# Softmax sums: the reciprocal is taken before the turn, the turn stands between the two ranges of value products, and the scaling is ordered two row minima later

## The chip, the cores and the metric

The kernel runs on one core of one Trainium2 chip. The metric is the device time of one execution in microseconds (us). The engines: TensorE (PE; PEld is its weight load), VectorE (DVE), ScalarE (ACT), GpSimd (POOL), and SyncE (SP), whose queue issues all DMA transfers of this kernel. Each engine works its own instructions in the order in which they stand; an instruction that waits holds up what stands behind it on the same engine. [...]

## The reference

Attention for 4 batches, 8 heads, 576 positions and head size 64, with a decay bias made from running sums of `s`; then a gated feed-forward block with a spatial mixing matrix (moe1); then a channel-mix block (moe2). Cut to what matters here:

```python
scores = scale * q @ k.T                       # per batch and head: 576 x 576
cum = cumsum(maximum(s, 0))
scores = where(causal, -1e9, scores + minimum(-(cum[:, None] - cum[None, :]), 0))
scores = scores - scores.max(-1)
attn = exp(scores)
attn = attn / (attn.sum(-1) + 1e-9)            # the division that the change touches
x = attn @ v                                   # heads side by side: 512 columns
# moe1, per batch
h = gelu(x @ w_in); u, v = halves of h
v = layernorm(v) * g_ln
x = x + (u * (w_sg @ v + b_sg)) @ w_out
# moe2, over all tokens
k = relu(mix(x, mu_k) @ w_k); r = sigmoid(mix(x, mu_r) @ w_r)
out = r * ((k * k) @ w_v)
```

The kernel keeps x transposed (features on the partitions), so the row sums of the softmax divide along the free axis, and each needs to be spread over 64 partitions.

## The kernel before, in words

**Attention.** Heads are worked in 16 pairs; pair `pr` holds heads 2hp and 2hp+1 of batch b. The generator `attn_pair` loads q and k of each head (`kq`), splits them into a rounded part and a rest (so that a product takes two matmuls, L252 and L253), and then goes through nine score steps `(hh, i)`: (0,0) to (0,3) are the four 128-row blocks of the first head, (2,4) the last 64 rows of both heads together, (1,0) to (1,3) the second head. In a step PE writes the scores into a PSUM tile `sc` (two buffers), DVE adds the mask and takes the row minimum `mx` in one instruction (L277; its small second row reads the accumulator), ACT takes the exponential and writes the row's sum into a column of `sums` (L285), PE turns the block by matmuls with the identity into a PSUM tile `tp` (three buffers), and ACT or DVE copies it to `pt1` or `pt2` (L305 to L314). Since there are two `sc` buffers, the scores of step n+2 wait for the row minimum of step n.

**The division.** After the nine steps PE turns `sums` (128 rows, 9 columns) into `rt` (9 rows, 128 columns, L317), DVE adds 1e-9 (L319) and takes the reciprocal (L320), SP stores it to DRAM (`rdram`, L321) and loads it three times, broadcast over 64 partitions, into `rb` (128 x 576, L324 to L326). PE meanwhile computes the two ranges of value products `pv` (L338): range 0 is queries 0 to 255, range 1 queries 256 to 575; ACT copies each to `xT` (L340). DVE's multiplication of `xT` by `rb` (L352) is put off: `scale_pending` issues it during the next pair, after the row minimum of step `LATE`, here (0, 3), or at the start of a batch's moe1 for the pair that is its last.

**moe1 and moe2.** moe1 of batch b reads the four scaled `xT` of its batch (L386 to L389) and runs groups of matmuls (L368), named v, u, sg and o after what they compute; `wc`, `wcs`, `wy` are tiles of its weights and of their splitting on DVE and ACT. Its yields are interleaved with the attention of the batches ahead, so that from 60 to about 380 us most of PE's attention steps stand among moe1's matmuls. After it, moe2 (k, r, and products psa to psc) needs no attention.

**What sets the order.** The program's text gives one order; the framework's scheduler then reorders the instructions of each engine by its own estimates, with priorities, buffers and dependences as constraints. A change at one place can so move instructions of many others.

Of the kernel before, what the change touches and what calls it, by code (L numbers as in the profile page):

```python
# [8 lines left out]
F32 = mybir.dt.float32  # L9
# [5 lines left out]
B, H, S, D = 4, 8, 576, 64  # L15
DM, DFF = 512, 1024
FH = DFF // 2
P = 128
# [10 lines left out]
SUM_EPS = 1e-9  # L29
# [8 lines left out]
def fused_kernel(ctx, tc, kqT, vL, s, w_in, g_ln, w_sgT, b_sg, w_out, mu_k, mu_r, w_k, w_v, w_r, out):  # L38
    nc = tc.nc
# [10 lines left out]
    rdram = dram.tile([B * H // 2, 9, P], F32, tag="rdram", name="rdram")  # L50
    ident = const.tile([P, P], F32, tag="ident", name="ident")
# [43 lines left out]
    psum1 = banks1.enter_context(tc.tile_pool(name="psum1", bufs=3, space=bass.MemoryType.PSUM))  # L95
# [3 lines left out]
    at = ap_stack.enter_context(tc.tile_pool(name="at", bufs=2, side="right"))  # L99
# [16 lines left out]
    with tc.high_priority():  # L116
# [20 lines left out]
        out=mask[:, 512:], in_=mask[:, 512:], pattern=[[-1, P]], compare_op=ALU.is_ge,  # L137
# [70 lines left out]
    def attn_pair(b, hp):  # L208
        pr = b * (H // 2) + hp
        first = b == 0  # L210
        ops = []
        for hh in range(2):
# [5 lines left out]
            i = hd % (NSET + 1) if first else hd % NSET  # L218
# [25 lines left out]
        sm = sums[pr % 2]  # L244
# [12 lines left out]
        for hh, i in steps:  # L257
# [8 lines left out]
            for ci, (c0, c1) in enumerate(chunks):  # L266
# [5 lines left out]
                else:  # L272
# [5 lines left out]
                    out=st[:, c0:c1], in0=sc[:, :n], in1=mk, op0=ALU.add, op1=ALU.min,  # L278
# [10 lines left out]
            exps.append(e)  # L289
            if (hh, i) == LATE:  # L290
                scale_pending(mi)
# [5 lines left out]
            tag = "acc" if first and i > 2 else "tp"  # L297
            tp = psum1.tile([P, 512], F32, tag=tag, name=f"tp{pr}_{hh}_{i}", bufs=3)
# [14 lines left out]
                    nc.scalar.copy(pt2[:, a, :4, q0 - QS:], tp.rearrange("p (j a m) -> p a j m", j=4, a=2)[:, a])  # L313
                nc.vector.tensor_copy(pt2[:, :, 3, 0:64], tp4[:, :P].rearrange("p (a m) -> p a m", a=2))  # L314
            yield (i + 1) * 200
        rt = psum1.tile([P, 512], F32, tag="tp", name=f"rt{pr}", bufs=3)
        nc.tensor.transpose(rt[:9, :P], sm, ident)  # L317
        rc = at.tile([9, P], F32, tag="rc", name=f"rc{pr}")
        nc.vector.tensor_scalar_add(rc, rt[:9, :P], SUM_EPS)  # L319
        nc.vector.reciprocal(rc, rc)  # L320
        nc.sync.dma_start(out=rdram[pr], in_=rc)  # L321
        rbs = at.tile([P, S], F32, tag="rb", name=f"rb{pr}", bufs=2)
        rq = rdram[pr].rearrange("i q -> (i q)")
        nc.sync.dma_start(out=rbs[:64], in_=rq[:S].partition_broadcast(64))  # L324
        nc.sync.dma_start(out=rbs[64:, :512], in_=rq[S + 64:].partition_broadcast(64))
        nc.sync.dma_start(out=rbs[64:, 512:], in_=rq[S:S + 64].partition_broadcast(64))  # L326
        for r in range(2):
            q0, n = ((0, QS), (QS, S - QS))[r]
            acc = psum1.tile([P, 512], F32, tag="acc", name=f"pv{pr}_{r}", bufs=3)
            nk = 2 if r == 0 else NT  # L330
            for kk in range(nk):
                o = max(0, kk * P - q0)
                for a in range(2):
                    if r == 0:
                        pt = pt1[:, a, :QS] if kk == 0 else pt1[:, a, QS:]
                    else:
                        pt = pt2[:, a, kk, o:] if kk < 4 else pt2[:, a, 3, 0:64]
                    nc.tensor.matmul(acc[64 * a:64 * a + 64, o:n], vf[:, a, kk], pt, start=(kk == 0), stop=(kk == nk - 1))  # L338

            nc.scalar.copy(x_t[:, q0:q0 + n], acc[:, :n])  # L340
            yield 4000
# [6 lines left out]
    def scale_pending(early):  # L348

        while pending:  # L350
            x_t, rbs = pending.pop()
            i = nc.vector.tensor_tensor(out=x_t, in0=x_t, in1=rbs, op=ALU.mult)  # L352
            if early is not None:
                after(i, early)
# [156 lines left out]


    pairs = [attn_pair(b, h) for b in range(B) for h in range(H // 2)]

    def a_stream():
# [4 lines left out]
                yield total  # L520
            yield 2 * n + 2.0

    LATE = (0, 3)
    A_COST = 2 * 3136 + 6600 + 8000 + 128
    E_COST = V_W * 56 * 512 + U_W * 8 * 12 * 288 + O_W * 8 * 12 * 288 + S_W * 8 * 14 * 288
    LEAD = 1
# [334 lines left out]
```

## Time and profile before

| | |
|---|---|
| median of 3 runs | 683.07 us (681.43 to 684.61) |
| the profiled execution | 684.48 us, span 682.7 us, mean granted clock 0.988 |
| PE busy | 645.9 us (95%), 3912 matmuls |
| DVE busy | 478.4 us (70%), 995 instructions |
| ACT busy | 415.9 us (61%), 940 instructions |
| POOL busy | 220.1 us (32%), 233 instructions |

Shares are of the span. The span leaves out 1.8 us around the first and the last instruction of the profiled execution. The chain that ended last is 77% PE and 8% DVE. The kernel has three stretches with a different limit: attention alone up to about 60 us, attention among moe1's matmuls up to about 380 us, and matmuls without attention after it.

### The profile page before, as it was taken

Reading aid. Unit: us, or ns where it says so; the run is one execution under the profiler, and the core shown is the slowest. Engines: PE = TensorE matmul, PEld = TensorE weight load, DVE = VectorE, ACT = ScalarE, POOL = GpSimd, SP = SyncE. Lnnn points to the kernel's source line nnn. Section 1 sums busy time; section 2 is a strip of 40 time slices with the busy share of each in tenths; the row PEclk is TensorE's granted clock in tenths of the full one; section 3 lists DMA queues with packets and bytes.
Section 4 is the critical chain, followed back from the end, with each engine's and each line's share of the span. In section 5 each row is a group of like instructions: output and inputs, shape, how many; then the busy total and the mean of one; then the engine's idle time right before and its main releaser. Section 6 shows DMA issues by size and latency. Waiting matters only on the chain.

```text
span 682.7 us, 11530 instructions
## 1 busy us (share of the span) xinstructions
PE 645.9 (95%) x3912; PEld 554.7 (81%) x3912; DVE 478.4 (70%) x995; ACT 415.9 (61%) x940; POOL 220.1 (32%) x233
## 2 busy tenths in 40 slices
PE   2879999899999999999999998999999999999997
PEld 1557676779978988877988898988888988999997
DVE  6876679986568645479543488777865969677773
ACT  4978777785458656268633374577754778543430
POOL 8556646368437468247462030000000000000000
PEclk9979999999999999999999999999999999999999
DMA  7764662454553532833511764566745594455643
GB/s 218 216 207 144 180 169 76 142 162 149 161 185 90 163 93 55 263 91 103 152 33 49 254 229 142 170 212 224 249 143 184 169 359 152 160 187 179 238 139 116
DMA packets 56459, 112.74 MB, mean 165 GB/s; under 512 B 7680, under 2 KB 20624, under 8 KB 56400
## 3 DMA queue, kind: packets, MB, share of 16 engines
q1 hardware_dynamic: 56400, 112.01, 52.0%
q8 instruction: 31, 0.51, 0.3%
q14 instruction: 28, 0.23, 0.1%
HBM read 74.46 MB, written 28.02 MB: 150 GB/s over the span
## 4 chain that ended last, share of the span: by engine, by line
PE 77%; DVE 8%; DMA 7%; ACT 2%; issue 2%; SPq 2%; POOL 1%; DVEq 0%; ACTq 0%; POOLq 0%
PE k L368 15%; PE sg L368 9%; PE r L368 7%; PE pv L338 7%; PE psa L770 7%; PE o L368 5%; PE tp L303 5%; PE u L368 4%; PE sc L252 4%; PE v L368 4%; PE psb L770 4%; PE sc L253 3%; DMA lraw<-in_w_k_dram 2%; PE psc L770 2%; DMA kq<-in_kqT_dram 2%
## 5 line engine op out<-in xcount | busy, mean ns | idle before, releaser
L368 PE MATMUL k<-x,wk 128*128 128x512 f32 (+1 forms) x480 | 101.4, 372 | 0.0
L368 PEld LDWEIGHTS k<-x,wk 128*128 128x128 f32 x480 | 83.6, 188 | 17.4
L252 PE MATMUL sc<-ka,qa 128*128 128x512 f32 (+3 forms) x180 | 63.6, 363 | 23.2 <-DMA ka<-ka 12.4
L285 ACT ACTIVATE st<-st,mx 128x128 f32<-128x128 f32 (+4 forms) x124 | 72.0, 582 | 19.8 <-DVE mx L277 19.2
L277 DVE CUSTOM_DVE_ANT_0 st<-sc,mask 128x512 f32<-128x512 f32 (+3 forms) x124 | 61.0, 502 | 27.8 <-PE sc L253 24.6
L368 PE MATMUL sg<-wsg,vn 128*128 128x288 f32 x448 | 67.0, 303 | 3.5 <-DVE vn L69 2.6
L368 PEld LDWEIGHTS sg<-wsg,vn 128*128 128x128 f32 x448 | 62.3, 192 | 4.3 <-DVE vn L69 2.9
L338 PE MATMUL pv<-pt,vf 128*64 128x320 f32 (+4 forms) x448 | 64.7, 366 | 0.2 <-ACT pt L305 0.2
L252 PEld LDWEIGHTS sc<-ka,qa 128*128 128x128 f32 x180 | 33.9, 189 | 33.2 <-DVE mx L277 14.4
L253 PE MATMUL sc<-KB,QB 128*128 128x512 f32 (+3 forms) x180 | 57.1, 333 | 0.9 <-DMA KB<-crt 0.9
L338 PEld LDWEIGHTS pv<-pt,vf 128*64 128x64 f32 x448 | 35.4, 136 | 23.5 <-issue 5.2
L303 PE MATMUL tp<-ident,st 128*128 128x128 f32 x300 | 49.5, 282 | 1.6 <-ACT st L285 1.5
L368 PE MATMUL r<-x,wr 128*128 128x512 f32 (+1 forms) x240 | 50.6, 372 | 0.0
L368 PEld LDWEIGHTS r<-x,wr 128*128 128x128 f32 x240 | 41.7, 188 | 8.8
L368 PE MATMUL v<-wv,xs 128*128 128x512 f32 x192 | 48.4, 397 | 0.0
L69 POOL TENSOR_TENSOR qa<-kq,QB 64x576 fp32r<-64x576 f32 x29 | 45.1, 1555 | 4.5 <-ACT QB L229 2.3
L229 POOL CAST QB<-kq 64x576 fp32r<-64x576 f32 x28 | 21.2, 761 | 74.1 <-PE sc L253 44.8
L303 PEld LDWEIGHTS tp<-ident,st 128*128 128x128 f32 x300 | 35.6, 142 | 11.0 <-ACT st L285 5.1
L69 POOL TENSOR_TENSOR KB<-kq,ka 64x576 fp32r<-64x576 f32 x29 | 42.7, 1474 | 3.4 <-ACT ka L230 1.4
L368 PE MATMUL o<-gh,wc 128*128 128x288 f32 x192 | 40.8, 298 | 0.7 <-DMA wc<-wscr 0.7
L368 PEld LDWEIGHTS v<-wv,xs 128*128 128x128 f32 x192 | 35.1, 188 | 7.5 <-POOL QB L229 0.5
L368 PE MATMUL u<-xs,wc 128*128 128x288 f32 x288 | 40.8, 297 | 0.0
(188 smaller groups left out, 1451.3 us busy)
## 6 DMA issues: line engine op xcount, KB each, us to landing
wc<-wscr SPq DMA_DIRECT2D x24, 512.0 KB
kq<-in_kqT_dram SPq DMA_DIRECT2D x32, 288.0 KB
kr<-kdram SPq DMA_DIRECT2D x12, 768.0 KB
kdram<-k SPq DMA_DIRECT2D x16, 512.0 KB
yt<-ydram SPq DMA_DIRECT2D x24, 257.0 KB
vf<-in_vL_dram SPq DMA_DIRECT2D x16, 320.0 KB
ydram<-y SPq DMA_DIRECT2D x16, 288.5 KB
gt<-gdram SPq DMA_DIRECT2D x12, 384.0 KB
```

What stands on the lines that cost most here:

```text
L69: eng.tensor_tensor(out=lo, in0=x, in1=f32(hi), op=ALU.subtract)
L229: (nc.scalar.copy if hd < 2 else nc.gpsimd.tensor_copy)(qb[64:128], kq[64:128])
L252: nc.tensor.matmul(sc[:m, :c1 - c0], qa[:, q], ka[:, c0:c1], start=True, stop=False)
L253: nc.tensor.matmul(sc[:m, :c1 - c0], qb[:, q], kb[:, c0:c1], start=False, stop=True)
L277: mi = nc.vector.tensor_tensor_reduce(out=st[:, c0:c1], in0=sc[:, :n], in1=mk, op0=ALU.add, op1=ALU.min, scale=-SCALE, scalar=mx[:, 0:1] i ...
L285: e = nc.scalar.activation(st[:, :w], st[:, :w], AF.Exp, bias=mx[:, last:last + 1], scale=-1.0, accum_out=sm[:, i + 5 * (hh == 1):i + 5 * ...
L303: nc.tensor.transpose(tp[:, c:c + P], st[:, j * P:(j + 1) * P], ident)
L338: nc.tensor.matmul(acc[64 * a:64 * a + 64, o:n], vf[:, a, kk], pt, start=(kk == 0), stop=(kk == nk - 1))
L368: nc.tensor.matmul(acc, a, w_, start=(i == 0), stop=(i == n - 1))
L770: nc.tensor.matmul(ps[:, c, :HW], l, r, start=(start and i == 0), stop=(i == len(mms) - 1), skip_group_check=True)
```

## The change

Epsilon and reciprocal are now applied to `sums` as it stands, 128 rows by 9 columns (`rs`, new L317 and L318). The new `spread()` has PE turn `rs` (L323), ACT copy the turned tile from PSUM to `rc` (L325, sixteen new ACT instructions in all), and SP store and load as before (L326 to L330). It is called between the two ranges of value products. `LATE` becomes (1, 0): the scaling follows the row minimum of the next pair's step (1, 0), two steps behind (0, 3). Below the change, lines have numbers seven higher (L338 is L345, L352 is L359, L368 is L375, L389 is L396).

```diff
--- before.py
+++ after.py
@@ -313,18 +313,25 @@
                     nc.scalar.copy(pt2[:, a, :4, q0 - QS:], tp.rearrange("p (j a m) -> p a j m", j=4, a=2)[:, a])
                 nc.vector.tensor_copy(pt2[:, :, 3, 0:64], tp4[:, :P].rearrange("p (a m) -> p a m", a=2))
             yield (i + 1) * 200
-        rt = psum1.tile([P, 512], F32, tag="tp", name=f"rt{pr}", bufs=3)
-        nc.tensor.transpose(rt[:9, :P], sm, ident)
-        rc = at.tile([9, P], F32, tag="rc", name=f"rc{pr}")
-        nc.vector.tensor_scalar_add(rc, rt[:9, :P], SUM_EPS)
-        nc.vector.reciprocal(rc, rc)
-        nc.sync.dma_start(out=rdram[pr], in_=rc)
+        rs = at.tile([P, 9], F32, tag="rs", name=f"rs{pr}")
+        nc.vector.tensor_scalar_add(rs, sm, SUM_EPS)
+        nc.vector.reciprocal(rs, rs)
         rbs = at.tile([P, S], F32, tag="rb", name=f"rb{pr}", bufs=2)
-        rq = rdram[pr].rearrange("i q -> (i q)")
-        nc.sync.dma_start(out=rbs[:64], in_=rq[:S].partition_broadcast(64))
-        nc.sync.dma_start(out=rbs[64:, :512], in_=rq[S + 64:].partition_broadcast(64))
-        nc.sync.dma_start(out=rbs[64:, 512:], in_=rq[S:S + 64].partition_broadcast(64))
+
+        def spread():
+            rt = psum1.tile([P, 512], F32, tag="tp", name=f"rt{pr}", bufs=3)
+            nc.tensor.transpose(rt[:9, :P], rs, ident)
+            rc = at.tile([9, P], F32, tag="rc", name=f"rc{pr}")
+            nc.scalar.copy(rc, rt[:9, :P])
+            nc.sync.dma_start(out=rdram[pr], in_=rc)
+            rq = rdram[pr].rearrange("i q -> (i q)")
+            nc.sync.dma_start(out=rbs[:64], in_=rq[:S].partition_broadcast(64))
+            nc.sync.dma_start(out=rbs[64:, :512], in_=rq[S + 64:].partition_broadcast(64))
+            nc.sync.dma_start(out=rbs[64:, 512:], in_=rq[S:S + 64].partition_broadcast(64))
+
         for r in range(2):
+            if r:
+                spread()
             q0, n = ((0, QS), (QS, S - QS))[r]
             acc = psum1.tile([P, 512], F32, tag="acc", name=f"pv{pr}_{r}", bufs=3)
             nk = 2 if r == 0 else NT
@@ -520,7 +527,7 @@
                 yield total
             yield 2 * n + 2.0
 
-    LATE = (0, 3)
+    LATE = (1, 0)
     A_COST = 2 * 3136 + 6600 + 8000 + 128
     E_COST = V_W * 56 * 512 + U_W * 8 * 12 * 288 + O_W * 8 * 12 * 288 + S_W * 8 * 14 * 288
     LEAD = 1
```

The scheduler's orders differ in many places. Three of them follow, and a fourth in words.

On SP, at the end of pair 0: `kq5` is the q and k of head 5, `rdram` the store of the reciprocals of pair 0, `rb0` their three loads, `vf2` the values of pair 2. Before:

```order
L231 DMA qa4_532<-QB1_85 64x576
L321 DMA rdram_65<-rc0_298 9x128
L217 DMA kq5_543<-in_kqT_dram 128x576
L324 DMA rb0_302<-rdram_65 64x576
L325 DMA rb0_302<-rdram_65 64x512
L326 DMA rb0_302<-rdram_65 64x64
```

After:

```order
L231 DMA qa4_536<-QB1_85 64x576
L217 DMA kq5_547<-in_kqT_dram 128x576
L326 DMA rdram_65<-rc0_308 9x128
L239 DMA vf2_544<-in_vL_dram 128x640
L328 DMA rb0_299<-rdram_65 64x576
L329 DMA rb0_299<-rdram_65 64x512
L330 DMA rb0_299<-rdram_65 64x64
```

The load of `kq5` has moved ahead of the store of the reciprocals, and `vf2` between the store and the loads.

On DVE, in pair 4, where pair 3 is scaled (`xT3` by `rb3`; `mx4_2_4` and `mx4_1_0` are row minima of pair 4, `pt2_4` a copy of a turned block). Before:

```order
L277 ISA st4_2_4_948,mx4_2_4_949<-sc4_2_4_1_956,mask2_123,mx4_2_4_949 128x64
L277 ISA mx4_2_4_949 128x1
L307 COPY pt2_4_903<-tp4_0_3_942 128x4x128
L352 TENSOR_TENSOR xT3_708<-xT3_708,rb3_840 128x576
L277 ISA st4_1_0_974,mx4_1_0_975<-sc4_1_0_0_976,mask_83 128x128
L277 ISA mx4_1_0_975 128x1
```

After:

```order
L277 ISA st4_2_4_956,mx4_2_4_957<-sc4_2_4_1_964,mask2_123,mx4_2_4_957 128x64
L277 ISA mx4_2_4_957 128x1
L359 TENSOR_TENSOR xT3_714<-xT3_714,rb3_843 128x576
L307 COPY pt2_4_911<-tp4_0_3_950 128x4x128
L277 ISA st4_1_0_982,mx4_1_0_983<-sc4_1_0_0_984,mask_83 128x128
L277 ISA mx4_1_0_983 128x1
```

The scaling now stands ahead of the copy to `pt2_4`; both still stand ahead of the minimum of step (1, 0), whose row comes after.

On DVE, in pair 6, where pair 5 is scaled (`u0`, `v0`, `vn0` are gates of moe1 of batch 0; `wcs3`, `wcs4`, `wy4_0` weights being split). Before:

```order
L419 TENSOR_SCALAR v0_1022<-v0_1022,mv0_1024,rstd0_1025 64x512
L352 TENSOR_TENSOR xT5_1150<-xT5_1150,rb5_1360 128x576
L82 SCALAR_TENSOR_TENSOR wy4_0_1456<-wr4_0_1455,wy4_0_1456 128x256
L499 SCALAR_TENSOR_TENSOR u0_1_1419<-u0_1_1419,u0_1_1_1437 128x288
L69 TENSOR_TENSOR wcs3_1399<-wy3_1_1410,wcs3_1399 128x256
L84 SCALAR_TENSOR_TENSOR wy4_0_1456<-wy4_0_1456 128x256
L307 COPY pt2_6_1520<-tp6_0_3_1577 128x4x128
L277 ISA st6_2_4_1621,mx6_2_4_1622<-sc6_2_4_1_1629,mask2_123,mx6_2_4_1622 128x64
L277 ISA mx6_2_4_1622 128x1
L277 ISA st6_1_0_1647,mx6_1_0_1648<-sc6_1_0_0_1649,mask_83 128x128
L277 ISA mx6_1_0_1648 128x1
```

After:

```order
L277 ISA mx6_2_4_1633 128x1
L69 TENSOR_TENSOR wcs3_1411<-wy3_1_1422,wcs3_1411 128x256
L84 SCALAR_TENSOR_TENSOR wy4_0_1468<-wy4_0_1468 128x256
L506 SCALAR_TENSOR_TENSOR u0_1_1431<-u0_1_1431,u0_1_0_1432 128x288
L69 TENSOR_TENSOR vn0_0_1034<-v0_1030,vn0_0_1034 64x512
L506 SCALAR_TENSOR_TENSOR u0_1_1431<-u0_1_1431,u0_1_1_1449 128x288
L508 SCALAR_TENSOR_TENSOR u0_1_1431<-u0_1_1431,u0_1_0_1432 128x288
L307 COPY pt2_6_1532<-tp6_0_3_1588 128x4x128
L69 TENSOR_TENSOR wcs4_1466<-wy4_0_1468,wcs4_1466 128x256
L277 ISA st6_1_0_1658,mx6_1_0_1659<-sc6_1_0_0_1660,mask_83 128x128
L277 ISA mx6_1_0_1659 128x1
L359 TENSOR_TENSOR xT5_1160<-xT5_1160,rb5_1367 128x576
```

The second minimum of step (2, 4) (its accumulator read is the first row) has moved ahead of the two weight operations `wcs3` and `wy4_0`; the minimum of step (1, 0) stays behind them and more; the scaling has moved behind that minimum.

On PE, in pair 8, the score steps of the second head stood apart among moe1's o groups of batch 0: `sc8_1_1` and `sc8_1_2` between o0_2_0 and o0_2_1, `sc8_1_3` ahead of v1_0. Now `sc8_1_1` stands in the last o group, `sc8_1_2` and `sc8_1_3` inside v1_0, and the first four score steps of pair 9 follow directly.

## Rows read from the trace of the kernel before

**Rows 1.** Windows: stretch, length, busy us (instructions) per engine; PEclk is the granted clock

```profile
38.00:48.20 10.20, 7.77 (x28) 6.02 (x28) 8.56 (x25) 7.00 (x20) 4.61 (x5) 0.50 0.67 208
...
60.00:96.00 36.00, 35.17 (x228) 24.93 (x226) 24.04 (x68) 28.85 (x82) 18.24 (x17) 1.00 0.55 154
...
96.00:133.50 37.50, 32.72 (x203) 25.72 (x201) 33.59 (x73) 26.61 (x69) 21.24 (x24) 1.00 0.39 114
...
133.50:137.00 3.50, 3.50 (x16) 3.42 (x15) 2.97 (x11) 3.06 (x11) 0.00 (x0) 0.51 0.47 158
...
160.00:380.00 220.00, 219.15 (x1496) 187.32 (x1495) 131.12 (x345) 120.73 (x309) 116.46 (x123) 1.00 0.40 118
```

**Rows 2.** Waits of PE, 20 to 160 us: total us, times, longest

```profile
PE sc L252 <- DVE mx L277: 11.2, 10, 3.3
```

**Rows 3.** Waits of PE, 160 to 680 us

```profile
PE sg L368 <- DVE vn L69: 2.6, 1, 2.6
```

**Rows 4.** Waits of DVE, 20 to 160 us

```profile
DVE xT L352 <- DMA rb<-rdram: 5.1, 5, 2.1
```

**Rows 5.** Groups of DVE by form: busy us, mean ns of one, idle before

```profile
L320 DVE RECIPROCAL rc<-rc 9x128 f32<-9x128 f32 x16 | 15.0, 937 | 0.3
...
L319 DVE TENSOR_SCALAR rc<-rt 9x128 f32<-9x128 f32 x16 | 4.3, 271 | 0.7 <-PE rt L317 0.7
...
L416 DVE BATCH_NORM_AGGREGATE mv<-st 128x2 f32<-128x6 f32 x16 | 2.7, 170 | 0.2
...
L62 DVE TENSOR_SCALAR mu<-mu 128x8 f32<-128x8 f32 x1 | 1.1, 1108 | 1.7 <-DMA mu<-in_mu_r_dram 1.7
```

**Rows 6.** Timeline of SP, pair 0: start us, duration us, line, operation

```profile
31.59 0.31 SPq L321 DMA_DIRECT2D rdram<-rc  x1
...
32.00 0.35 SPq L217 DMA_DIRECT2D kq<-in_kqT_dram  x1
```

**Rows 7.** Timeline of DVE, pairs 0 and 1: start, duration, idle before

```profile
30.62 0.94 DVE L320 RECIPROCAL rc<-rc 9x128 f32<-9x128 f32 x1
...
36.62 0.96 DVE L230 CAST ka_f<-kq 64x576 fp32r<-64x576 f32 x1 [1.21 <-DMA kq<-in_kqT_dram]
...
39.71 1.83 DVE L352 TENSOR_TENSOR xT<-xT,rb 128x576 f32<-128x576 f32 x1 [1.11 <-DMA rb<-rdram]
```

**Rows 8.** Timeline of PE after that

```profile
38.44 0.58 PE L252 MATMUL sc<-ka,qa 128*128 128x256 f32 x1 [2.54 <-DVE mx L277]
...
43.14 0.80 PE L252 MATMUL sc<-ka,qa 128*128 128x512 f32 x1 [1.99 <-DVE mx L277]
```

**Rows 9.** Timeline of ACT, pair 0, the first product copied from PSUM

```profile
31.97 0.38 ACT L340 COPY xT<-pv 128x256 f32<-128x256 f32 x1
```

**Rows 10.** Timeline of DVE, pairs 3 and 4

```profile
79.56 0.69 DVE L307 COPY pt<-tp 128x512 f32<-128x512 f32 x1 [1.56 <-PE tp L303]
...
81.37 0.76 DVE L352 TENSOR_TENSOR xT<-xT,rb 128x576 f32<-128x576 f32 x1 [1.12 <-DMA rb<-rdram]
```

**Rows 11.** Timeline of DVE, pairs 5 and 6

```profile
126.47 0.76 DVE L352 TENSOR_TENSOR xT<-xT,rb 128x576 f32<-128x576 f32 x1 [0.51 <-DMA rb<-rdram]
...
128.33 1.27 DVE L69 TENSOR_TENSOR wcs<-wy,wcs 128x256 fp32r<-128x256 f32 x1
...
129.52 1.61 DVE L84 SCALAR_TENSOR_TENSOR wy<-wy 128x256 uint32<-128x256 uint32 x1
...
131.66 0.27 DVE L277 CUSTOM_DVE_ANT_0 st<-sc,mask,mx 128x64 f32<-128x64 f32 x1
...
133.63 0.42 DVE L69 TENSOR_TENSOR wcs<-wy,wcs 128x256 fp32r<-128x256 f32 x1
```

**Rows 12.** Timeline of POOL beside it

```profile
127.84 1.48 POOL L69 TENSOR_TENSOR KB<-kq,ka 64x576 fp32r<-64x576 f32 x1
...
129.39 1.46 POOL L69 TENSOR_TENSOR qa<-kq,QB 64x576 fp32r<-64x576 f32 x1
```

**Rows 13.** Timeline of PE beside it

```profile
131.99 0.38 PE L252 MATMUL sc<-ka,qa 128*128 128x256 f32 x1 [3.32 <-DVE mx L277]
```

## Prediction

> **What bounds the kernel now.** I read the page's busy shares first, then windows cut where the granted clock or the mix of work changes, then PE's waits, and then timelines around the longest of them. PE is busy for 95% of the span, so a part of VectorE's work can pay only where PE waits for VectorE. The windows show where that is. From 160 to 380 us, where pairs 8 to 15 are worked among moe1's matmuls, PE is busy for 219.15 of 220 us [rows 1]; behind 160 us its longest entry in the waits is 2.6 us, for a tile of moe1 [rows 3]. There even a free division would give at most 0.85 us. From 20 to 160 us PE waits 11.2 us, in ten waits, for the row minimum `mx` [rows 2], and VectorE is busy for 33.59 of 37.5 us between 96 and 133.5 us [rows 1]. Three of the ten make up 2.54 + 1.99 + 3.32 = 7.85 us [rows 8, 13]. Behind two long pauses stand the stretches at half clock, 38 to 48.2 us (granted 0.50) and 133.5 to 137 us (0.51) [rows 1]: PE's pause came first, then the lower level. In 20 to 160 us VectorE also waits 5.1 us, in five waits, for the loads of `rb` [rows 4].
>
> **The change, part by part.** All durations are from the profiled execution, 684.48 us (span 682.7 and 1.8 around it). It is 1.4 us above the median of 683.07; sums are made against 684.48, and 1.4 is taken off at the end.
>
> *The smaller reciprocal.* Each pair loses an addition of 271 ns and a reciprocal of 937 ns on 9 x 128 [rows 5], 1.21 us of VectorE, and gains two operations on 128 x 9. The trace has no such operation. The nearest are 128 x 2 from 128 x 6 at 170 ns, and a single 128 x 8 at 1,108 ns [rows 5]. I take 170 ns, since that is a mean over 16 and the other ran once. The relief is 1.21 - 0.34 = 0.87 us a pair; between the ends it is +0.87 to -1.0 us. Sixteen pairs make 13.9 us of VectorE, but only the seven pairs worked before 160 us (0 to 6) can hand any to PE, 6.1 us at most, and each only if nothing else is late at its next wait.
>
> *The turn between the ranges.* PE's turn now needs `rs`, so it can wait for VectorE; where it stands behind the first range, matmuls already issued cover it. The sixteen copies on ScalarE are new. The first product copied from PSUM, 128 x 256, took 0.38 us [rows 9]; a copy of 9 x 128 lies between nothing and that, I take 0.3 us, 4.8 us in all. ScalarE is busy for 120.73 of 220 us behind 160 us [rows 1], which hides it there. In the early pairs it is also a delay: in pair 0 the new copy stands behind the copy that starts at 31.97 and lasts 0.38 [rows 9], so `rc` is ready at about 32.65 instead of 30.62 + 0.94 = 31.56 [rows 7]. That is 1.1 us later, although VectorE's part is finished sooner. No term for PE follows yet; it returns with the scaling.
>
> *SP at the end of pair 0.* The store of `rc` was issued at 31.59, and the load of `kq5` stood behind it at 32.00 [rows 6]. VectorE then waited 1.21 us for that load, until 36.62 [rows 7], and PE waited 2.54 us for the minimum behind it [rows 8]. The load now stands ahead of the store, so its issue no longer waits for the reciprocals. VectorE's 1.21 us go, and what is late next is VectorE's own queue: -1.2 us on PE's path, bounds 0 and -2.54. The store waits behind one more issue and `vf2` stands before the loads of `rb0`, which adds 0.3 to 0.6 us to them by the issue times [rows 6].
>
> *The scaling of pair 0.* It waited 1.11 us for `rb` and took 1.83 us from 39.71 [rows 7]; then the minimum for which PE waited 1.99 us came [rows 8]. With `rc` 1.1 us later and the scaling one minimum and two weight operations later, `rb` and the scaling are again due together, at about 40.7. I take 0, bounds -1.99 and +1.1.
>
> *The scaling of pair 3.* In the new order it stands ahead of the copy to `pt2_4`, not behind it. VectorE was free at 79.56 - 1.56 = 78.0; the copy ran at 79.56 while the loads travelled, and the scaling ran at 81.37 [rows 10]. Now VectorE waits from 78.0 to about 81.4 for `rb`, then scales, then copies (0.69 us), and the minimum of step (1, 0) comes 0.69 us later, the copy itself 2.6 us. PE has moe1's matmuls there (35.17 of 36 busy [rows 1]) but its order is fixed too: +0.7 us, bounds 0 and +2.6.
>
> *The scaling of pair 5.* It started at 126.47 after a wait of 0.51 us; with other work behind it the second minimum of step (2, 4) came at 131.66, and PE stood for 3.32 us until 131.99 [rows 11, 13]. That minimum now comes before `wcs3` and `wy4_0`, which took 1.27 and 1.61 us [rows 11], so this wait should go. What is late next is the minimum of step (1, 0), for which the scores two steps on wait. The scaling (0.76 + 0.51) has left its path and the relief of pair 5 (0.87) helps, 2.1 us together; but four instructions that ran behind it, from about 132.2 to 133.63 + 0.42 [rows 11], now run ahead of it, 1.9 us. It comes about when it came; PE has done two short steps more by then, but the step after waits for the scaling and one more minimum. I take -0.5 us, bounds -3.32 and +1.5.
>
> *The rest.* The other seven of the ten waits sum to 11.2 - 7.85 = 3.35 us [rows 2], in pieces that mostly end with a row minimum not far behind a division; I take -0.3 us, bounds 0 and -1.7. The closer bunch of score steps in pair 8 takes away some of the matmuls that stood between; PE idles 0.85 us in the whole stretch today [rows 1], so it can only lose: +0.3 us, bounds 0 and +4, the upper end if the two steps moved into v1_0 each wait for a whole exponential chain of about 2 us (scores, minimum and exponential, an estimate).
>
> Sum: -1.2 + 0 + 0 + 0.7 - 0.5 - 0.3 + 0.3 = -1.0. That gives 683.5 against 684.48, and about 682.0 beside the median.
>
> [...] VectorE's `wcs3` took 1.27 us at 128.33 while GpSimd ran tensor operations from 127.84 and 129.39 [rows 11, 12]; the same shape took 0.42 us at 133.63 [rows 11], in a window in which GpSimd did nothing [rows 1]. [...]
>
> **The rivals.**
>
> *The waits fall in a row, 675.* If VectorE's relief adds up over pairs, half of the 11.2 us goes (-5.6). Where a pause shortens, the clock may stay up: at full clock 38 to 48.2 us would take half of PE's 7.77 busy us (3.9) less, and 133.5 to 137 half of 3.5 (1.75) [rows 1]; one of the two, on average 2.8. 684.48 - 8.4 - 1.4 = 674.7. For it: PE's longest pauses end with VectorE. Against: the minimum for step (1, 0) of pair 6 keeps its place in time, and pair 0's scaling too.
>
> *The scaling takes over as the wait, 688.* VectorE works in order, so a scaling whose `rb` is not there holds up the row minima behind it. Its place moved by two minima, but `rc` now comes by way of PE and ScalarE, 1.1 us later in pair 0. Today VectorE waits 5.1 us for `rb` in seven pairs [rows 4]. If each `rb` comes 1.1 us later against its scaling, 7.7 us more are waited; with the 3.4 us of pair 3 and half of it passed on to PE, 5 us, and no relief left: 684.48 + 5 - 1.4 = 688. It decides from the point where waits for `rb` before 160 us exceed about 9 us. For it: rows 10. Against: two minima and their gaps are mostly longer than 1.1 us.
>
> *The change does nothing to PE, 683.* Each pause ends on another VectorE instruction at the same time. The fixed order of moe1's weight work speaks for it, the moved load of `kq5` against it.
>
> *The small operations are stretched by GpSimd, 683.5.* By the overlap seen at 128.33, a VectorE operation that meets GpSimd's lasts 1.27 - 0.42 = 0.85 us more. GpSimd works about half of 20 to 160 us; fourteen small operations, seven of them met, cost 6 us, which eats the 6.1 us of relief, and the later `rc` costs some tenths. For it: `wcs3`. Against: the old reciprocal's mean.
>
> **How the numbers follow.** Forecast 0.40 (its own range 679 to 686), waits falling 0.23, scaling as the wait 0.21, nothing 0.09, stretched 0.07. A change under 0.5%, 3.4 us here, can't be told from none. Faster than 679.7: the second case, and a quarter of the first, 0.33. Slower than 686.5: nearly all of the third and a little of the first, 0.22. Within: 0.45. The range runs from 674.5 to 688, which leaves out half of the two outer cases, about 0.2.
>
> **What would show it.** The row minima's share of PE's waits before 160 us should fall from 11.2 to about 9 us, with the 3.32 us of pair 6 moved on to the next steps. VectorE's busy time should fall by about 14 us, ScalarE's rise by about 5. The pause of 2.54 us should be near 1.3. Waits for `rb` should stand near 8 us before 160 us. The small operations should take 0.17 us each. PE's idle time from 160 to 380 us should stay under 2 us. I am wrong if both stretches at half clock are gone (then it is faster), if PE's idle time grows in pair 3 or 8 by more than 2 us, or if the small operations take near 1 us.

## The result, and the profile after

The changed kernel takes 688.17 us (median of 16 runs, 686.37 to 691.59). The kernel before, run as often beside it, takes 686.51 us (679.59 to 689.79; its first three runs, known ahead of the prediction, had 683.07). The ratio is 1.0054, 95% interval 1.0035 to 1.0073; it is not the quotient of the two medians, which is 1.0024 (that of the means is 1.0044). So the change makes the kernel slower, by 1.7 us between the medians and by 3.7 us by the ratio, where a gain of 1.0 us, to 682.0, was forecast. Of the 6.2 us between 682.0 and 688.17, 3.4 lie in the kernel before, which took 686.51 us here and not 683.07. The third case of the prediction has this sign, but its 688 was met only with these 3.4 us, and, as will be seen, by another mechanism. Ratios and their intervals leave out executions in a slower state of the chip; the medians do not (one of e16's twelve below).

The profiled execution took 687.20 us, span 685.4. The page's first part of the changed kernel:

```profile
PE 643.6 (94%) x3912; PEld 551.1 (80%) x3912; DVE 483.4 (71%) x995; ACT 418.4 (61%) x956; POOL 222.8 (32%) x233
```

The smaller reciprocal should have taken 14 us from VectorE; VectorE is busy for 5.0 us more (478.4 before). PE is busy for 2.3 us less and idle for 5.0 us more, which makes the span's 2.7. The windows (stretch, length, busy us per engine; PEclk is the granted clock as a share of the full one), as in [rows 1]:

```profile
38.00:48.20 10.20, 6.49 (x29) 4.88 (x31) 10.05 (x23) 7.12 (x19) 5.13 (x5) 0.64 0.60 183
60.00:96.00 36.00, 31.14 (x198) 21.16 (x198) 21.10 (x69) 27.38 (x79) 19.31 (x17) 1.00 0.50 134
96.00:133.50 37.50, 33.82 (x217) 27.98 (x213) 32.00 (x73) 27.49 (x68) 18.43 (x23) 1.00 0.40 119
133.50:137.00 3.50, 2.87 (x19) 2.45 (x19) 2.98 (x7) 2.70 (x12) 2.47 (x2) 1.00 0.83 224
160.00:380.00 220.00, 218.46 (x1477) 184.48 (x1477) 133.39 (x348) 123.90 (x323) 119.61 (x122) 1.00 0.41 116
```

Most of the loss stands between 60 and 96 us: PE idles 36 - 31.14 = 4.86 us there, 0.83 before. Another 1.7 us stand between 20 and 60 us (10.18 us idle, 8.50 before). Between 96 and 133.5 us PE idles 3.68 instead of 4.78, and the half-clock stretch behind it is gone (1.00 for 0.51); half of its 3.5 us, 1.75 by estimate, is most of what PE's busy time fell by. The first half-clock stretch has only moved: the granted clock is now 0.50 from 41 to 51 us, so that the window from 38 us shows 0.64. What PE waited for from 20 to 160 us (total, times, longest), as in [rows 2]:

```profile
PE sc L252 <- DVE mx L277: 7.7, 11, 2.7
PE tp L303 <- ACT st L285: 4.1, 6, 1.2
PE rt L323 <- DVE rs L318: 3.3, 2, 2.4
PE v L375 <- ACT xs L393: 1.5, 1, 1.5
PE u L375 <- DVE v L508: 1.4, 1, 1.4
```

The row minima fell from 11.2 to 7.7, as forecast and a little more. Three waits that were not there or small took their place: PE's turn for VectorE's `rs` (3.3), a turned block for the exponential (4.1, was 1.5), and moe1's first v group for the scaled tile (1.5). The second of these before:

```profile
PE tp L303 <- ACT st L285: 1.5, 3, 0.7
```

The operations of the division by form on VectorE (busy us, mean ns of one, idle before), and the scaling in the kernel before:

```profile
L359 DVE TENSOR_TENSOR xT<-xT,rb 128x576 f32<-128x576 f32 x16 | 19.0, 1190 | 10.1 <-DMA rb<-rdram 10.1
L317 DVE TENSOR_SCALAR rs<-sums 128x9 f32<-128x9 f32 x16 | 10.4, 653 | 4.2 <-ACT st L285 4.1
L318 DVE RECIPROCAL rs<-rs 128x9 f32<-128x9 f32 x16 | 3.3, 208 | 0.2
```

```profile
L352 DVE TENSOR_TENSOR xT<-xT,rb 128x576 f32<-128x576 f32 x16 | 14.4, 900 | 23.0 <-DMA rb<-rdram 19.5 <-ACT xT L340 3.0 <-ACT st L285 0.5
```

The reciprocal is as small as hoped (208 ns). The addition takes 653 ns on the mean, 156 at least and 1,373 at most, and the scaling rose from 900 to 1,190 ns. Of the 19.3 us of the old addition and reciprocal [rows 5], 13.7 are left, and the scaling takes 4.6 more. That is 1.0 us less in all; the other 6.0 us come, in sum, from VectorE operations of unchanged shape that lasted longer in the new order, the steps L82 and L84 on `syt` alone 4.1 us (14 operations, 10.6 us before, 14.8 now). Pair 0 shows how the addition became long. VectorE, then GpSimd, then PE of the changed kernel, from start and duration:

```profile
27.37 1.37 DVE L317 TENSOR_SCALAR rs<-sums 128x9 f32<-128x9 f32 x1
28.66 0.67 DVE L277 CUSTOM_DVE_ANT_0 st_f<-sc,mask 128x512 f32<-128x512 f32 x1
29.27 0.07 DVE L277 DVE_READ_ACCUMULATOR2_ANT mx<- 128x1 f32 x1
29.27 1.80 DVE L84 SCALAR_TENSOR_TENSOR syt<-syt 128x512 uint32<-128x512 uint32 x1
31.00 0.20 DVE L318 RECIPROCAL rs<-rs 128x9 f32<-128x9 f32 x1
```

```profile
26.61 2.11 POOL L69 TENSOR_TENSOR KB<-kq,ka 64x576 fp32r<-64x576 f32 x1
```

```profile
27.50 1.40 PE L345 MATMUL pv<-pt,vf 128*64 128x256 f32 x10
31.34 0.27 PE L323 MATMUL rt<-ident,rs 128*9 128x128 f32 x1 [2.44 <-DVE rs L318]
...
38.15 0.39 PE L252 MATMUL sc<-ka,qa 128*128 128x256 f32 x1 [0.93 <-DVE mx L277]
...
42.59 0.80 PE L252 MATMUL sc<-ka,qa 128*128 128x512 f32 x1 [2.66 <-DVE mx L277]
```

The addition ends at 28.74, 0.02 us behind GpSimd's operation (28.72). It is so with each of the ten that lasted over 0.5 us: all start while GpSimd runs and end 0.02 to 0.04 us behind it; the six short ones (0.16 to 0.18 us) have no GpSimd operation at their start, or one that is just ending. The kernel before held such a case already, the row of 1,108 ns in [rows 5]. VectorE, then GpSimd, of the kernel before:

```profile
12.36 1.11 DVE L62 TENSOR_SCALAR mu<-mu 128x8 f32<-128x8 f32 x1 [1.65 <-DMA mu<-in_mu_r_dram]
```

```profile
12.05 1.40 POOL L69 TENSOR_TENSOR KB<-kq,ka 64x576 fp32r<-64x576 f32 x1
```

It ends at 13.47, 0.02 us behind GpSimd's 13.45.

Behind the addition of pair 0 a minimum and a weight operation stand before the reciprocal in VectorE's order, and PE, which has done the first range (27.50 to 28.90), waits 2.44 us for `rs`. The pause of 2.54 us in [rows 8] fell to 0.93.

In pair 3, the last of batch 0, whose scaled tile moe1 needs, the timelines of PE (the turn, and moe1's v group), of ScalarE (the copy), of SP (the store and the first load), of VectorE (the scaling) and of GpSimd:

```profile
74.83 1.40 PE L345 MATMUL pv<-pt,vf 128*64 128x256 f32 x10
...
76.91 0.27 PE L323 MATMUL rt<-ident,rs 128*9 128x128 f32 x1
...
87.33 0.73 PE L375 MATMUL v<-wv,xs 128*128 128x512 f32 x2 [1.48 <-ACT xs L393]
```

```profile
77.65 0.25 ACT L325 COPY rc<-rt 9x128 f32<-9x128 f32 x1
```

```profile
77.93 0.30 SPq L326 DMA_DIRECT2D rdram<-rc  x1
...
80.23 0.47 SPq L328 DMA_DIRECT2D rb<-rdram  x1
```

```profile
84.75 1.82 DVE L359 TENSOR_TENSOR xT<-xT,rb 128x576 f32<-128x576 f32 x1 [2.27 <-DMA rb<-rdram]
```

```profile
84.55 1.41 POOL L69 TENSOR_TENSOR qa<-kq,QB 64x576 fp32r<-64x576 f32 x1
```

Before, the first value product and the store of pair 3:

```profile
73.36 1.40 PE L338 MATMUL pv<-pt,vf 128*64 128x256 f32 x10
```

```profile
75.36 0.30 SPq L321 DMA_DIRECT2D rdram<-rc  x1
```

The scaling starts at 84.75; before, at 81.37 and with 0.76 us [rows 10]. It is 3.4 us later, of which 1.5 were lost ahead of the pair's first value product (74.83 us, 73.36 before); the turn behind those products and ScalarE's copy make 1.1 more by the store (77.93, 75.36 before), and the loads are 0.8 longer on their way. VectorE idles for 2.27 us in front of the scaling, and the copy to `pt2_4`, whose block PE had turned by 83.61, stands behind it until 86.50. The scaling, begun 0.2 us after an operation of GpSimd, lasts 1.82 us, and v waits.

### The profile page after: what moved, and what is told of

Its sections match the earlier page's. It is cut to its first block, busy times and chain, and to the rows that moved or that the text cites. A ratio compares the mean times of both kernels' runs of the same rounds, so it can differ in the third digit from the quotient of the medians.

```text
span 685.4 us, 11545 instructions
## 1 busy us (share of the span) xinstructions
PE 643.6 (94%) x3912; PEld 551.1 (80%) x3912; DVE 483.4 (71%) x995; ACT 418.4 (61%) x956; POOL 222.8 (32%) x233
## 5 line engine op out<-in xcount | busy, mean ns | idle before, releaser
L375 PE MATMUL k<-x,wk 128*128 128x512 f32 (+1 forms) x480 | 101.4, 372 | 0.0
L375 PEld LDWEIGHTS k<-x,wk 128*128 128x128 f32 x480 | 83.6, 188 | 17.4
L345 PE MATMUL pv<-pt,vf 128*64 128x320 f32 (+4 forms) x448 | 66.3, 371 | 0.9 <-DVE pt L307 0.5
L375 PE MATMUL sg<-wsg,vn 128*128 128x288 f32 x448 | 65.4, 298 | 1.7 <-DVE vn L69 1.7
L375 PEld LDWEIGHTS sg<-wsg,vn 128*128 128x128 f32 x448 | 60.7, 188 | 2.3 <-DVE vn L69 1.9
L345 PEld LDWEIGHTS pv<-pt,vf 128*64 128x64 f32 x448 | 35.6, 138 | 24.7 <-issue 6.4
L375 PE MATMUL v<-wv,xs 128*128 128x512 f32 x192 | 49.3, 398 | 1.5 <-ACT xs L393 1.5
L375 PE MATMUL r<-x,wr 128*128 128x512 f32 (+1 forms) x240 | 50.6, 372 | 0.0
L375 PEld LDWEIGHTS r<-x,wr 128*128 128x128 f32 x240 | 41.7, 188 | 8.8
L69 POOL TENSOR_TENSOR qa<-kq,QB 64x576 fp32r<-64x576 f32 x29 | 46.7, 1611 | 3.7 <-ACT QB L229 1.6
L375 PE MATMUL u<-xs,wc 128*128 128x288 f32 x288 | 42.1, 298 | 1.6 <-DVE vx L420 0.6
L375 PEld LDWEIGHTS v<-wv,xs 128*128 128x128 f32 x192 | 34.9, 188 | 9.5 <-ACT xs L393 1.7
L375 PEld LDWEIGHTS u<-xs,wc 128*128 128x128 f32 x288 | 39.1, 188 | 3.3 <-issue 1.5
L375 PE MATMUL o<-gh,wc 128*128 128x288 f32 x192 | 40.8, 298 | 0.0
```

What stands on the lines that cost most here:

```text
L69: eng.tensor_tensor(out=lo, in0=x, in1=f32(hi), op=ALU.subtract)
L375: nc.tensor.matmul(acc, a, w_, start=(i == 0), stop=(i == n - 1))
```

## The experiments

Seventeen runs, each median over 9 to 12 executions; ratios are to the kernel before on the same chip, with 95% intervals. "Idle" is PE's idle time from 60 to 100 us in the one profile of each (0.83 before, 4.86 in the changed kernel); two profiles of one kernel differ in it by up to 1 us (e4 and e15, e13 and e17).

| run | edit | median us | ratio | idle us |
|---|---|---|---|---|
| e4 | before, scaling behind (1, 0) | 680.14 | 0.9951 (0.9919 to 0.9984) | 1.83 |
| e15 | the same again | 681.18 | 0.9959 (0.9929 to 0.9989) | 0.86 |
| e10 | before, division between the ranges | 686.90 | 1.0029 (1.0000 to 1.0059) | 1.50 |
| e11 | both of these | 683.71 | 0.9995 (0.9963 to 1.0028) | 1.73 |
| e8 | changed, turn written ahead of both ranges, scaling behind (0, 3) | 688.15 | 1.0054 (1.0023 to 1.0084) | 5.06 |
| e2 | changed, scaling behind (0, 3) | 686.52 | 1.0047 (1.0012 to 1.0082) | 4.95 |
| e3 | changed, turn written ahead of both ranges | 690.03 | 1.0090 (1.0057 to 1.0123) | 3.72 |
| e12 | changed, again | 688.39 | 1.0075 (1.0044 to 1.0106) | 4.88 |
| e1 | changed, no addition | 683.09 | 0.9981 (0.9951 to 1.0012) | 2.35 |
| e6 | no addition, scaling behind (0, 3) | 684.98 | 1.0018 (0.9987 to 1.0049) | 2.97 |
| e5 | changed, three reciprocals | 686.06 | 1.0034 (1.0011 to 1.0057) | 3.16 |
| e7 | e4, no addition | 682.87 | 0.9984 (0.9959 to 1.0009) | 2.05 |
| e9 | changed, addition with unequal patterns | 686.39 | 1.0036 (1.0014 to 1.0057) | 4.25 |
| e16 | changed, copy of `rc` by VectorE | 684.26 | 1.0001 (0.9975 to 1.0028) | 4.14 |
| e13 | e9 and e16 together | 680.59 | 0.9943 (0.9915 to 0.9971) | 2.30 |
| e17 | the same again | 681.87 | 0.9965 (0.9940 to 0.9991) | 3.07 |
| e14 | e16, no addition | 688.41 | 1.0058 (1.0026 to 1.0090) | 4.35 |

**The three parts.** e10 and e4 make one part alone, e2 and e11 two of them. e8 was to make the first part alone, and e3 the first and the third; both write the turn ahead of both ranges. e2 and e4 set `LATE`; e3 calls the new function once ahead of the loop (e8 does so too, with `LATE = (0, 3)`):

```diff
+        spread()
         for r in range(2):
-            if r:
-                spread()
```

e10 and e11 wrap the old turn, addition, reciprocal, store and loads into such a function and call it between the ranges.

e2: 

> The changed kernel with the scaling back behind the row minimum of step (0, 3). Theory C, the later scaling costs (moe1 of batch 0 waits 1.5 us for the last scaled tile at 87 us, and the scaling itself met GpSimd more often, mean 1.19 us against 0.90): the ratio goes to 0.996 to 1.002, the wait of the v group for xs is gone. Theories A and B: waits of VectorE for rb grow from 10.1 us to above 15, ratio 1.004 to 1.012.

e3: 

> The changed kernel with the turn issued ahead of both ranges of value products, where it stood before; reciprocal first and scaling late as in the change. Theory B, the place of the turn: ahead of the products PE's wait for rs has no matmuls in front of it, so the wait grows from 3.3 us to above 5 and the ratio to 1.008 or more. If the place is worth nothing, 1.003 to 1.008.

e4: 

> The kernel before with only the scaling moved behind step (1, 0). Theory C: slower by 0.2 to 0.6 percent, with a wait of the v group for xs near 87 us. Theories A and B: no change, or faster by up to 0.4 percent, since 19.5 us of VectorE's waits for rb shrink to about 10.

e8: 

> The first part of the change alone: reciprocal of the unturned sums with the addition, then the turn ahead of both ranges, the copy by ScalarE, the scaling behind step (0, 3). Theory A: slower than before by what the stretched addition and PE's wait for it cost, 1.004 to 1.011. If the three parts add up (turn between the ranges -0.4, later scaling 0 to -0.5 percent), 1.008 to 1.013.

e10: 

> The old division (turn the sums, add and reciprocal on 9 x 128 from PSUM, on VectorE) moved as a whole between the two ranges of value products; scaling behind step (0, 3). The turn needs only the exponentials here. By theory A and B the place costs little by itself: 0.998 to 1.004, with rb later and more waits of VectorE for it than the 19.5 us of the kernel before.

e11: 

> The same with the scaling behind step (1, 0), so the change without its first part. If the first part is what made the change slower, this is faster than the kernel before, 0.992 to 0.999; if the place of the turn costs, 1.001 or more.

The later scaling (theory C) is not what costs: alone it makes the kernel before faster by 0.4 to 0.5% (e4, e15), with VectorE's waits for `rb` at 12.7 us in e4 for 19.5, and in the changed kernel its undoing changes nothing beyond the intervals (e2, where PE still waits 1.5 us for `xs`).

The scheduler undid the edit of e8 and e3. By the traces, the instructions of every engine stand in e8 in the order of e2, and in e3 in the order of the changed kernel but for one turn, its copy and its store, near 170 us. So e8 is e2 once more, and e3 nearly the changed kernel once more. They show how far apart the ratios of one order can lie in different runs (1.0047 and 1.0054; 1.0054, 1.0075 and 1.0090), and not what the place of the turn is worth on the new division, which no run here shows.

On the old division the place of the turn costs 0 to 0.6% (e10), and 0.4% with the later scaling (e4 and e15 to e11), neither well beyond the intervals. The first part costs 0.2%, inside the intervals, with the scaling behind (0, 3) (e10 to e2 and e8), and 0.6 to 0.95% with the later scaling (e11 to the changed kernel, e12 and e3).

**The addition.** e1, e6 and e7 leave out the addition of 1e-9; e5 puts two more reciprocals in its place.

e1: 

> Leaves out the addition of 1e-9 (a row's largest exponential is 1, so each sum is at least 1 and the addition changes no bit of it in f32); all else as the changed kernel. Theory A, the sixteen additions stretched by GpSimd (10.4 us of VectorE where 2.6 were forecast) are what made the change slower: their 10.4 us go, PE's two waits for rs (3.3 us before 100 us) shrink to under 1.5, and the time falls to the kernel before or below it (ratio 0.992 to 1.000). Theory B, the loss is PE's turn and the later scaling in the new order, whatever the addition costs: the ratio stays at 1.003 to 1.008.

e5: 

> The changed kernel with the addition replaced by two more reciprocals (three in a row give the reciprocal again). Theory A, the addition costs because GpSimd's operations stretch it, and the reciprocal is of a kind that they don't stretch: 48 reciprocals at 0.2 us are 9.8 us of VectorE, about what addition and reciprocal take in the changed kernel (13.7), but none is over 0.25 us, and the ratio comes near that of the kernel without the addition (0.9981), 0.997 to 1.002. If any third operation in front of the turn costs as much, by its mere place in VectorE's order, the ratio stays at 1.004 or more.

e6: 

> Without the addition and with the scaling back behind step (0, 3). If leaving out the addition is worth the same 0.7 percent as with the later scaling, the ratio is 0.995 to 1.000 (the same edit with the addition was at 1.0047). If the gain came from that order alone, it is at 1.003 or more.

e7: 

> The kernel before with the scaling behind step (1, 0), and the reciprocal taken straight from the turned sums in PSUM, without the addition. The addition there reads PSUM and takes 0.271 us, never stretched, so theory A expects little: ratio 0.991 to 0.997 against 0.9951 with the addition. If an instruction less on the way is what pays, it goes to 0.990 or below.

Without the addition the changed kernel is 0.7% faster (e1), and with the scaling behind (0, 3) 0.3%, inside the intervals (e6). On the old division it pays nothing (e7). e5 was to tell stretch from place and came out between: its three reciprocals took 0.208 to 0.211 us on the mean, yet 1.0034. All four also reorder the program, so a run was needed in which nothing but the stretch differs.

**The same order, without the stretch.** e9 gives the addition an output of three by three columns with a gap:

```diff
-        nc.vector.tensor_scalar_add(rs, sm, SUM_EPS)
-        nc.vector.reciprocal(rs, rs)
+        rp = at.tile([P, 12], F32, tag="rp", name=f"rp{pr}")
+        nc.vector.tensor_scalar_add(rp.rearrange("p (a b) -> p a b", b=4)[:, :, :3], sm.rearrange("p (a b) -> p a b", b=3), SUM_EPS)
+        nc.vector.reciprocal(rs.rearrange("p (a b) -> p a b", b=3), rp.rearrange("p (a b) -> p a b", b=4)[:, :, :3])
```

e9: 

> The changed kernel with one access pattern altered: the addition writes its nine columns as 3 by 3 with a gap, where it reads nine in a row; the reciprocal reads them back from there. Every engine's order of instructions is that of the changed kernel. In the changed kernel each stretched addition ends 0.03 us behind the GpSimd operation that ran when it began. [...] Theory B, the stretch hardly matters and the loss is the chain through VectorE in front of PE's turn: additions unstretched or not, the ratio stays at 1.004 or more and PE still waits over 2.5 us for rs.

e12: 

> The changed kernel once more, beside the one with unequal patterns on the same chip: 1.004 to 1.007.

By the traces every engine's order in e9 is that of the changed kernel. The two operations by form in e9, then the addition of pair 0 with GpSimd beside it, and PE's wait:

```profile
L319 DVE RECIPROCAL rs<-rp 128x9 f32<-128x9 f32 x16 | 3.4, 210 | 0.2
L318 DVE TENSOR_SCALAR rp<-sums 128x9 f32<-128x9 f32 x16 | 2.5, 154 | 4.2 <-ACT st L285 4.1
```

```profile
27.61 0.15 DVE L318 TENSOR_SCALAR rp<-sums 128x9 f32<-128x9 f32 x1
```

```profile
26.84 2.11 POOL L69 TENSOR_TENSOR KB<-kq,ka 64x576 fp32r<-64x576 f32 x1
```

```profile
PE rt L324 <- DVE rs L319: 1.7, 2, 0.9
```

GpSimd runs the same operation over the addition, and the addition takes 0.15 us instead of 1.37; all sixteen lie at 145 to 164 ns. VectorE is busy for 475.8 us, 7.6 less. PE's wait for `rs` halves, and the median falls by 2.0 us beside e12 on the same chip. The stretch is shown, and so is that it costs time: 0.39% between the ratios here (the means are 0.2 to 0.5% apart, 95% interval), and once more 0.36% between e16 and e17 on one chip (1.0001 and 0.9965; means 0.2 to 0.6% apart). e13, the same kernel as e17 on another chip, has 0.9943. e16 and these two also stand in one order but for one row of ScalarE and one of VectorE. The addition reads nine columns in a row in both kernels; it writes nine in a row in the changed kernel (156 to 1,373 ns) and three by three with a gap in e9 (145 to 164 ns). Why the pattern of the output makes this difference, no run shows.

The stretch is not the whole loss, and hardly the part between 60 and 96 us. PE idles 4.25 us there in e9 too (4.88 in e12), and moe1's v group waits as before:

```profile
86.40 0.73 PE L376 MATMUL v<-wv,xs 128*128 128x512 f32 x2 [1.49 <-ACT xs L394]
```

What e9 gains in idle time lies mostly elsewhere: 9.12 us from 20 to 60 us (9.98 in e12, 8.50 before) and 3.88 from 96 to 160 us (5.16 in e12, 6.07 before).

**The copy on ScalarE.** With the stretch gone 0.36% were left (interval 0.14 to 0.57). e13, e14 and e16 have `nc.vector.tensor_copy(rc, rt[:9, :P])` in place of `nc.scalar.copy`.

e13: 

> The changed kernel with the unstretched addition (ratio 1.0036) and the turned tile copied from PSUM by VectorE, not ScalarE. If what is left of the loss is the hop through ScalarE's queue (the copy behind exponentials, so rb and the scaled tile that moe1 of batch 0 waits for 1.5 us are late), the ratio falls to 0.996 to 1.001 and that wait goes. If it is the two chained VectorE operations ahead of PE's turn, it stays at 1.002 to 1.007, with PE's wait for rs (1.7 us) still there.

e14: 

> The same copy by VectorE, and no addition at all (the kernel without it, copy by ScalarE, was at 0.9981). If both matter, 0.993 to 0.997 and as fast as the kernel before with the later scaling; if the copy's engine is worth nothing, 0.996 to 1.001.

e15: 

> The kernel before with only the later scaling, once more: if its 0.9951 was no accident of that chip, 0.992 to 0.998.

e16: 

> The changed kernel with one edit: VectorE, not ScalarE, copies the turned tile from PSUM. Its order of instructions is that of the run at 0.9943, whose addition had unequal patterns; here the addition is stretched again. If the stretch costs about 2 us here too, the ratio is 0.996 to 1.000; if it is hidden in this order, 0.993 to 0.996. Either way, if the copy on ScalarE's queue was the rest of the loss, it is well below the changed kernel's 1.0054, and the wait of moe1's first v group for xs (1.5 us) is gone or under 0.5 us.

e17: 

> The kernel with unequal patterns in the addition and the copy by VectorE once more: 0.991 to 0.998 if its 0.9943 holds.

In the changed kernel this one line takes the slowdown away (e16: 1.0001), and with the unequal patterns the kernel is faster than before by 0.3 to 0.6% (e13, e17). PE's wait for `xs` is 0.4 us in e16 and e17, and gone in e13; in e13 PE's wait for `rs` is one:

```profile
PE rt L324 <- DVE rs L319: 0.7, 1, 0.7
```

But it is not the engine of the copy alone. Without the addition the same line makes the kernel slower, from 0.9981 (e1) to 1.0058 (e14), which has a wait for `xs` of 1.8 us again:

```profile
84.75 0.73 PE L374 MATMUL v<-wv,xs 128*128 128x512 f32 x2 [1.84 <-ACT xs L392]
```

Moving the copy makes the scheduler place hundreds of instructions anew (between e9 and e13, 386 of PE's 3,912 rows stand elsewhere by the traces). PE's idle time from 60 to 100 us follows the ratios loosely: 3.2 to 5.1 us in the kernels at 1.0034 to 1.0090, 3.1 and less in the others, but for e16 (4.14 us at 1.0001). The wait for `xs` does not decide it either: in e3, which has the changed kernel's order there, PE waited 0.2 us for `xs`, and the ratio is 1.0090. What remains open is how much of the remaining 0.4% is the hop through ScalarE and how much the order around pairs 3 and 4; no run here changes the hop and keeps the order.

Several expectations were missed. e7, e13 and e14 came outside all ranges named for them (0.9984, 0.9943, 1.0058), and e4 a little beyond its own (0.9951 for at most 0.4% faster). e5, e6 and e11 came between the ranges that were named. e9 came a little under the 1.004 of theory B (1.0036), and its 1.7 us of waiting for `rs` lie well under the 2.5 named there. e12 had 1.0075 for 1.007 at most.

## Why the prediction was wrong, point by point

- *The bound.* Right: what was won or lost lay where PE waits, before 160 us. PE's idle time from 160 to 380 us is 1.54 us, under the 2 that were named.
- *The smaller reciprocal.* This term failed in size. The relief of 0.87 us a pair took 170 ns for each of the two operations. The reciprocal has 208, the addition 653, so the relief is 1.21 - 0.86 = 0.35, and in pair 0, by 1.37 + 0.20, below zero. The row chosen was that of an operation which took at most 183 ns, GpSimd running or not; the row set aside, 1,108 ns, was a stretched one, as shown above, and the better guide to nearly half of the additions. The rival of stretched operations, given 0.07, named what the additions then did. It took the same for the reciprocal, against which it had the old one's mean of 937 ns itself (all sixteen took 924 to 942 ns, seven of them begun while GpSimd ran), and its price (all relief lost, 683.5) left out that PE waits for the chain.
- *The turn between the ranges.* This is the step that failed: "where it stands behind the first range, matmuls already issued cover it". In pair 0 the first range was done at 28.90 and PE waited until 31.34. Before, PE's turn needed only the exponentials, and VectorE's work on the division lay behind it, beside the value products. Now addition, minimum, weight operation and reciprocal stand one behind the other on VectorE, from 27.37 to 31.20, in front of PE's turn at 31.34. A part of the division that had been hidden came onto PE's path, 3.3 us before 160 us (1.7 without the stretch, in e9); the sum had no term for it. ScalarE's copy was sized rightly (0.249 us for 0.3), and `rc` of pair 0 was stored 0.6 us later (32.17 for 31.59), where 1.1 was forecast.
- *SP at the end of pair 0.* The term holds, though not by the pause that it named. That pause fell from 2.54 to 0.93 us (1.3 forecast), but the matmul behind it starts only 0.29 us earlier (38.15 for 38.44): held up for `rs`, PE came there 1.3 us later, and found less left to wait. In e9, with the shorter hold-up, the pause is as forecast and the matmul starts 1.4 us earlier:

```profile
37.01 0.58 PE L252 MATMUL sc<-ka,qa 128*128 128x256 f32 x1 [1.36 <-DVE mx L277]
```

- *The scaling of pairs 0, 3 and 5.* Pair 0: the pause of 1.99 became 2.66, where 0 was the term and +1.1 its bound; yet the matmul behind it starts 0.55 us earlier (42.59 for 43.14), since PE came there sooner, at a granted clock of 0.98 from 38 to 41 us (0.50 before). Pair 3: its region went wrong far beyond the +0.7 and its bound of 2.6 (idle +4.0 us between 60 and 96 us); the late `rb`, the stretched scaling and moe1's wait for it are part of that. Over 2 us there is one of the signs of being wrong that the prediction had named. Pair 5: the wait of 3.32 us is gone and no equal one follows it; PE's idle time from 96 to 160 us fell by 0.7 us (6.07 to 5.41), where -0.5 was the term, and the half-clock stretch behind the wait went with it.
- *The rest.* The +0.3 for the stretch behind 160 us came out as +0.7 (1.54 us idle for 0.85).
- *The third rival, 688.* The time came near it by luck: 3.4 us of it are the kernel before. VectorE's waits for `rb` before 160 us, which it wanted above about 9 us, fell from 5.1 to 4.2 us. The scaling of pair 3 was late through the late value products, the late `rc` and GpSimd. Its price also read the 5.1 us as those of seven pairs, where [rows 4] counts five waits, and half of 7.7 + 3.4 us is 5.6, not 5.
- *The later scaling* was costed only pair by pair. Alone it is the good part of the change (0.9951 and 0.9959, e4 and e15); with the other two parts its gain is gone (1.0054 to 1.0090). That the first part takes 0.6 to 0.95% of this is read from e11, whose order differs in many places.

Of the loss, the stretch is shown by runs that keep the order, 0.36 to 0.39%. That the rest is the longer way through VectorE and ScalarE in front of PE's turn and of the scaling is argued from the waits, and stays open.

## What to carry to other kernels

An operation that is cheaper by itself can still be dearer in its new place: ask which engine now stands in front of which. Here PE stood 2.44 us for VectorE in pair 0. Before pricing a small VectorE operation by its own size, look in the trace for one like it that ran beside GpSimd: the 128 x 9 addition took up to 1,373 ns there, the same with a gap in its output 164 at most (e9), and the reciprocal of that shape 216 at most in both kernels. When a scheduler orders the program, first see whether an edit moved what it was to move, and compare variants that keep the order before believing a cause under half a percent.

## What the runs showed of the hardware

In the changed kernel the 128 x 9 addition took 156 to 1,373 ns with nothing of its own different; with the gap in its output it took 145 to 164 ns throughout in e9. The reciprocal of the same shape took 194 to 216 ns in the changed kernel, six of the sixteen beside a GpSimd operation that had begun before it and ended after it, and 205 to 211 ns on the mean in every run that has it. The scaling took 0.75 us at least and up to 2.00 when GpSimd began first: every one over 0.85 us, four in the kernel before and nine in the changed kernel, began while a GpSimd operation ran and ended 0.61 to 0.62 us behind it. With the later scaling its mean was 1,190 ns in the changed kernel (844 in e2, which has the earlier one), but 934 (e4) and 861 (e15) on the old division (900 before).
